# Four more head pairs of a sparse attention take their scores as side-by-side 64-row 32-bit matmuls, and the planner's constants are chosen anew

## The chip, the cores and the metric

The kernel runs on one core of one Trainium2 chip. The metric is device time in microseconds (us), as the median of several executions. The profile is of one execution on that core.

## What is computed

An attention with a threshold, followed by two feed-forward layers:

```python
scores = (q @ k.T) / sqrt(64)                      # 4 batches, 8 heads, 576 tokens, 64 wide
thresh = max(scores) - tau                         # per row
attn   = softmax(where(scores >= thresh, scores, -1e9))
x      = heads of (attn @ v) side by side          # 2304 tokens x 512
g      = relu(x @ w1_in) ** 2                      # 512 -> 2048
x      = g @ w1_out                                # 2048 -> 512
h      = x @ w2_in
out    = max(0.01 * h, h) @ w2_out
```

All arrays are 32-bit floats. With `tau` = 0.02 a score that lies just at the threshold decides whether an attention weight is kept, so the scores have to be nearly exact; that is why they are either taken as true 32-bit matmuls or from numbers split in a high and a low part.

## The kernel before, in words

The kernel writes all its work down as operations with the values they read and write (`op`, line 83), each with a due time `prio` and one or more engines that could do it, each at a cost in us. `order` (line 118) then simulates the engines once, ahead of the run, and so fixes the order of the instructions on every engine. Engine letters are T (TensorE), V (VectorE), A (ScalarE), G (GpSimd), S (the DMA queue on SyncE). Among the operations that could start, the one with the earliest due time is taken; an operation marked urgent keeps others from starting just before it; the weights `CFG["price"]` (line 190), one set for each stretch of the plan, say when an operation is left for another engine. On the chip each engine takes its instructions strictly in that order and waits by semaphores.

**Attention.** The 4 batches have 4 pairs of heads each, so there are 16 pairs (0 to 15), and every pair has 9 steps: four row tiles of 128 queries for each of the two heads, and one step for the last 64 queries of both heads. That makes 144 steps. `prep(n)` (line 465) loads pair n's queries, keys and values during pair n-1. `step(i)` (line 561) makes the 128 x 576 scores `s` in PSUM (two buffers for `s`; line 580 or 594), then, on the tile:

- line 602, VectorE: the row maximum, negated (`nb`); line 604, VectorE or GpSimd: the threshold `th`
- line 603, ScalarE: `e` = exp(s - max)
- line 609, VectorE: `e` = (s >= th) * e with the row sum; with it the PSUM buffer of `s` comes free
- lines 612 and 615: the reciprocal `r` of the sum

and `rest` (line 618) turns `e` into weights and transposes them. For pairs 0 to 3 (`nav`, not changed) this is a 32-bit transpose on TensorE (lines 634, 635). For pairs 4 to 15 the weights become two 16-bit tiles, a rounded high part and the remainder, in one of two ways: a scaling straight to the high part and line 656 on VectorE for the remainder; or, for the steps that `CFG["lb"]` lists by batch (step number modulo 8), a scaling in place, a rounding (line 652) and a subtraction (line 653), which VectorE or GpSimd may do. A DMA then transposes both (line 662). `values` (line 675) multiplies with V (line 690, or 695 for `nav`) and writes `xs` to `x1d` in DRAM: with line 710 on VectorE, or, for the pairs that `CFG["xsg"]` names, with a ScalarE copy (707) and a GpSimd addition (708).

**Two ways to the scores.** `CFG["nat"]` lists the pairs that take the first one:

```python
# a pair in nat (line 571 ff.): 32-bit, the 64-wide contraction in half the rows of the array
for g in range(2):
    rows = slice(g * D, (g + 1) * D)
    nc.tensor.matmul(ps.get()[r, g, 0:S2], lhsT=o.q2()[rows, a, q], rhs=o.k2()[rows, a], start=True, stop=True)
# every other pair (line 591 ff.): round 32-bit halves, high and low queries in the 128 rows
ops = [(r, q, kk[hh]) for hh, r, q in lhs for kk in (o.KH, o.KL)]
for k, (r, q, kk) in enumerate(ops):
    nc.tensor.matmul(ps.get()[r, g, 0:S2], lhsT=o.Q.get()[:, q], rhs=kk.get()[:, g_(g)], start=k == 0, stop=k == len(ops) - 1)
```

In the first way the queries lie twice, in rows 0 to 63 and 64 to 127; the upper rows hold the first 288 keys, the lower rows the other 288, and the two matmuls of a step (four in the ninth step) run side by side in the two halves of the array. The preparation is one scaling of 128 x 576 keys. In the second way a step is four matmuls of 128 rows by 288 columns (eight in the ninth step), and the preparation scales 128 x 1152 keys in a `wraw` buffer (lines 451 and neighbours), rounds the queries (two operations) and subtracts for their low part (two on 64 rows), rounds the keys (two) and subtracts (two): one operation against nine, beside a small memset (line 502). Queries and keys of such a pair pass through two of the three `wraw` buffers.

**Feed-forward.** `ffn` (line 717) does the first layer for the first 1792 tokens in blocks of 256, with 12, 12, 12 and 10 of 16 weight blocks (`nf`), alongside the attention: lines 743 (h) and 769 (y) fill TensorE between the scores. It starts once batch 0 is done, behind step 36. After the attention, lines 1173 and 1215 do the rest of the first layer, and lines 1062 and 1140 the second layer in a form with fewer products. `w_block` (line 351) and `single` (line 880) load and decode the weights.

Of the kernel before, what the change touches and what calls it, by code (L numbers as in the profile page):

```python
# [24 lines left out]

CFG = dict(
    price=[{'V': 4.26, 'A': 2.141, 'G': 1.969},
           {'V': 2.149, 'A': 0.525, 'G': 0.657},
           {'V': 1.817, 'A': 0.791, 'G': 0.994},
           {'V': 4.978, 'A': 0.359, 'G': 0.535},  # L30
           {'V': 1.875, 'A': 0.851, 'G': 2.206},
           {'V': 2.958, 'A': 1.093, 'G': 2.527},
           {'V': 3.025, 'A': 1.378, 'G': 3.11}],
    lead1=0.194, xsg0=[0, 1], lbm=8, lb=[[0, 1, 4, 6, 7], [1, 5], [4], [3, 7]], xsm=4, xsg=[1], dq=0.417, xu=True, pqk=-3.957, pd1=2.075,
    pex=0.67, pd2=1.854, ph=3.829, pl=-2.392, hu=False, bg=5.522, lead=4.309, w0=25.544, wstep=1.281, fend=1.014, tol=0.2, hor=-0.199,
    xlead=5.334, nb=3, eb=4, pb=3, ptb=3, kvb=3, nat=[0, 1, 2, 3, 4, 5], nav=4, two=False, vb=2, tmb=1, gb=2, xb=1, w2step=-2.074,
    nf=[12, 12, 12, 10], wo=2.034, wold=[0, 9, 10, 14, 16], yal=40.688, xl2=28.416, xp=5, sp=2.529, ws=-2.249, ww=28.906, zc=3.11, th=0.368,
    x2l=3.836, sg0=2.669, sgstep=1.117, zb=1.278, zin=0.923, zout=0.928, slack=0.02, slackd=1.05, wrb=3, r1b=1, xrb=1,
)


# [1317 lines left out]
```

## Time and profile before

| | |
|---|---|
| median of 3 runs | 1014.09 us (1008.28 to 1015.57) |
| the profiled execution, its own time | 1012.67 us |
| its span, first to last instruction | 1010.8 us (1.9 us lie around it) |
| mean granted TensorE clock | 0.988 of full speed |
| busy, share of the span | TensorE 95%, VectorE 83%, ScalarE 70%, GpSimd 37% |

Busy time of TensorE is the time covered by records of matmuls. A record lasts longer than the matmul keeps the next one from starting: rows of line 743 and 769 have records of 0.28 us that start 0.12 us apart. What a matmul costs is therefore read from start to start. The starts of line 602, one for each step, date the steps: step 36 (pair 4) is at 102 us, pair 5 at 131.3, pairs 6 to 9 lie from 162.4 to 276.8, and the last step starts at 451.7.

### The profile page before, as it was taken

To read this page: it belongs to the slowest core of one execution; us is meant where nothing else is said; L and a number is where in the kernel's file an instruction comes from. 1 tells how busy PE (TensorE), PEld (TensorE's weight loads), DVE (VectorE), ACT (ScalarE), POOL (GpSimd) and SP (SyncE) were. 2 spreads that over 40 slices of the span, in tenths; PEclk is the share of its full clock that TensorE was granted. 3 is DMA by queue.
4 is the path that set the end of the run, shared out by engine and by line. 5 is a ranking of instruction groups with operands and counts; after the bars stand their busy time and mean duration, and the time that the engine had idled before them with its cause. 6 is when DMAs were issued, how large, how long until landed. Compare 5 with 4: busy or idle time off the path is not lost.

```text
span 1010.8 us, 20761 instructions
## 1 busy us (share of the span) xinstructions
PE 963.6 (95%) x7436; PEld 831.2 (82%) x7436; DVE 834.7 (83%) x1948; ACT 704.1 (70%) x1361; POOL 377.4 (37%) x467
## 2 busy tenths in 40 slices
PE   7888799998999999999999999999999999999997
PEld 3444478898999988999978898778888888888897
DVE  6899898888999888874666999799979859858766
ACT  4877888878788689975566998767737536446343
POOL 4788888886877688951400000000100000000000
PEclk7999799999999999999999999999999999999999
DMA  7556799998989877766665563530020020010000
GB/s 175 162 167 174 192 189 188 184 179 177 181 168 182 166 155 148 152 122 192 194 197 165 177 195 119 168 103 20 1 85 2 1 85 2 2 64 1 22 23 22
DMA packets 199351, 123.79 MB, mean 122 GB/s; under 512 B 156880, under 2 KB 176976, under 8 KB 199248
## 3 DMA queue, kind: packets, MB, share of 16 engines
q1 hardware_dynamic: 198800, 122.10, 50.7%
q8 instruction: 59, 0.97, 0.4%
q10 hardware_dynamic: 448, 0.36, 0.2%
q14 instruction: 44, 0.36, 0.1%
HBM read 72.75 MB, written 17.83 MB: 90 GB/s over the span
## 4 chain that ended last, share of the span: by engine, by line
PE 61%; DVE 17%; ACT 9%; issue 5%; DMA 5%; POOL 2%; SPq 0%; DVEq 0%; ACTq 0%; POOLq 0%
PE y L1140 8%; PE y L1062 7%; PE h L1140 7%; PE h L1062 7%; PE h L743 6%; PE h L1173 6%; PE y L1215 6%; PE y L769 5%; DVE e L609 3%; DVE P L656 3%; DMA PT<-P 3%; DVE nb L602 3%; PE s L594 2%; PE o L690 2%; ACT e L603 2%
## 5 line engine op out<-in xcount | busy, mean ns | idle before, releaser
L609 DVE SCALAR_TENSOR_TENSOR e<-s,th,e 128x576 f32<-128x576 f32 x144 | 116.6, 811 | 22.0 <-ACT e L603 18.1
L603 ACT ACTIVATE e<-s,nb 128x576 f32<-128x576 f32 x144 | 106.0, 740 | 27.1 <-DVE nb L602 17.9
L602 DVE TENSOR_REDUCE nb<-s 128x1 f32<-128x576 f32 x144 | 106.7, 747 | 15.5 <-PE s L580 7.8
L656 DVE SCALAR_TENSOR_TENSOR P<-e,r,P 128x576 f16<-128x576 f32 x86 | 86.4, 1011 | 5.3 <-POOL P L622 2.8
L903 POOL MEMSET yo<- 128x128 f32 x5 | 1.0, 206 | 201.1 <-DVE b L1070 88.7
L690 PE MATMUL o<-PT,V 128*128 128x320 f16 (+1 forms) x432 | 61.5, 287 | 5.1 <-DVE vbound L535 3.1
L594 PE MATMUL s<-KH,Q 128*128 128x288 f32 x200 | 59.2, 314 | 6.2 <-DVE e L609 5.3
L1089 ACT ACTIVATE b<-b 128x1024 f32<-128x1024 f32 (+1 forms) x40 | 38.8, 971 | 33.1 <-DVE b L329 33.0
L1140 PEld LDWEIGHTS <-gh 128*128 128x128 f16 x560 | 54.5, 98 | 6.1
L329 DVE TENSOR_TENSOR b<-b 128x256 f32<-128x256 f32 (+1 forms) x120 | 45.4, 390 | 14.9 <-ACT b L1089 14.3
L318 ACT CAST gh<-b 128x384 f16<-128x384 f32 (+1 forms) x78 | 44.0, 564 | 19.1 <-DVE b L329 18.5
L594 PE MATMUL s<-KL,Q 128*128 128x288 f32 x200 | 55.9, 294 | 0.0
L580 PE MATMUL s<-KH,Q 64*128 64x288 f32 (+1 forms) x240 | 43.0, 483 | 12.3 <-DVE e L609 5.2
L690 PEld LDWEIGHTS <-V 128*128 128x128 f16 x432 | 39.0, 98 | 17.0 <-issue 6.1
L329 DVE TENSOR_TENSOR gl<-b,gh 128x384 f16<-128x384 f32 x80 | 48.9, 615 | 0.2 <-ACT gh L318 0.2
L318 ACT CAST xh<-xr 128x512 f16<-128x512 f32 (+3 forms) x65 | 36.9, 580 | 16.5 <-DVE xr L329 14.7
L331 POOL TENSOR_TENSOR gl<-r,gh 128x512 fp32r<-128x512 f32 x31 | 42.3, 1366 | 12.7 <-DMA x1d<-xs 6.0
L623 ACT ACTIVATE P<-e,r 128x576 f16<-128x576 f32 x53 | 40.5, 770 | 9.1 <-DMA PT<-P 4.5
L318 ACT CAST gh<-r 128x512 fp32r<-128x512 f32 (+1 forms) x72 | 43.4, 603 | 4.8 <-DVE r L1181 3.6
L594 PEld LDWEIGHTS s<-KH,Q 128*128 128x128 f32 x200 | 37.7, 189 | 10.8 <-DVE e L609 4.2
L329 DVE TENSOR_TENSOR gl<-r,gh 128x512 fp32r<-128x512 f32 (+1 forms) x44 | 31.4, 715 | 14.9 <-ACT gh L318 14.7
L604 POOL TENSOR_SCALAR th<-nb,ca 128x1 f32<-128x1 f32 x70 | 32.5, 466 | 24.4 <-DVE nb L602 16.6
(1130 smaller groups left out, 3523.5 us busy)
## 6 DMA issues: line engine op xcount, KB each, us to landing
wraw<-w SPq DMA_DIRECT2D x64, 512.0 KB, 4.3
wraw<-qT SPq DMA_DIRECT2D x20, 288.0 KB, 4.1
wraw<-kT SPq DMA_DIRECT2D x20, 288.0 KB, 4.1
out<-yo SPq DMA_DIRECT2D x18, 256.0 KB, 2.3
VA<-vv SPq DMA_DIRECT2D x32, 128.0 KB, 2.9
x2d<-yo SPq DMA_DIRECT2D x16, 256.0 KB, 3.2
xr<-x2d SPq DMA_DIRECT2D x4, 1024.0 KB, 6.0
y1d<-ys SPq DMA_DIRECT2D x14, 256.0 KB, 2.7
```

Of the source, the lines that this page charges most:

```text
L318: alts.append(("A", act(n, psum), lambda: nc.scalar.copy(o(), i()), kind))
L329: alts.append(("V", dve(n), lambda: nc.vector.tensor_tensor(out=o(), in0=a(), in1=b(), op=alu), kind + "*"))
L594: nc.tensor.matmul(ps.get()[r, g, 0:S2], lhsT=o.Q.get()[:, q], rhs=kk.get()[:, g_(g)], start=k == 0, stop=k == len(ops) - 1)
L602: op(("V", 0.75, lambda: nc.vector.tensor_reduce(out=nb.get(), in_=pv(), axis=AX.XY, op=ALU.max, negate=True)), [ps], [nb], i + CFG["pd1"] ...
L603: op(("A", 0.74, lambda: nc.scalar.activation(e.get(), pv(), AF.Exp, bias=nb.get(), scale=1.0)), [ps, nb], [e], i + CFG["pex"], True)
L609: op(("V", 0.82, lambda: nc.vector.scalar_tensor_tensor(out=e.get(), in0=pv(), scalar=th.get(), in1=e.get(), op0=ALU.is_ge, op1=ALU.mult, ...
L656: op(("V", 0.8, lambda: nc.vector.scalar_tensor_tensor(out=lo(), in0=ev(), scalar=r_.get()[:, k:k + 1], in1=hi(), op0=ALU.mult, op1=ALU.su ...
L690: nc.tensor.matmul(ps.get()[:, 0:w], lhsT=o.V16.get()[:, k if k < NH else k - NH, h].rearrange("p a d -> p (a d)"), rhs=parts16(pt)[:, k, ...
L743: nc.tensor.matmul(ps.get()[:, i], lhsT=a.get()[:, kc * P:(kc + 1) * P], rhs=x.get()[:, kc], start=(i == 0 and q == 0 and kc == 0), stop=( ...
L1062: nc.tensor.matmul(ps.get()[:, 0:w], lhsT=half(wt)[:, ct + kc * P:ct + (kc + 1) * P], rhs=xt(k)[:, kc], start=fresh and q == 0, stop=q == ...
L1140: nc.tensor.matmul(y.get()[:, c * h:(c + 1) * h], lhsT=l, rhs=r, start=first and c == 0 and q == 0, stop=last and c == len(ks) - 1 and q == 2)
L1173: nc.tensor.matmul(ps.get()[:, 0:n], lhsT=a.get()[:, kc * P:(kc + 1) * P], rhs=x.get()[:, kc, 0:n], start=(q == 0 and kc == 0), stop=(q == ...
```

## The change

Only constants change. `nat` gets pairs 6, 7, 8 and 9 beside 0 to 5. `lb` lists other and more steps: of the 36 steps of batch 1, 18 instead of 9 subtract for the remainder; of batch 2, 13 instead of 4; of batch 3, 18 instead of 9. `xsg` is emptied, so that pair 1 of each of the batches 1 to 3 (four `xs` tiles each) uses line 710 as well. `hu` and `xu` are marks of urgency: the scaling of `e` becomes urgent, and the making of `xs` no longer is. The rest are due times, prices and tolerances of the planner. `nf`, the numbers of buffers and `nav` stay.

```diff
     price=[{'V': 4.26, 'A': 2.141, 'G': 1.969},
-           {'V': 2.149, 'A': 0.525, 'G': 0.657},
-           {'V': 1.817, 'A': 0.791, 'G': 0.994},
-           {'V': 4.978, 'A': 0.359, 'G': 0.535},
-           {'V': 1.875, 'A': 0.851, 'G': 2.206},
-           {'V': 2.958, 'A': 1.093, 'G': 2.527},
-           {'V': 3.025, 'A': 1.378, 'G': 3.11}],
-    lead1=0.194, xsg0=[0, 1], lbm=8, lb=[[0, 1, 4, 6, 7], [1, 5], [4], [3, 7]], xsm=4, xsg=[1], dq=0.417, xu=True, pqk=-3.957, pd1=2.075,
-    pex=0.67, pd2=1.854, ph=3.829, pl=-2.392, hu=False, bg=5.522, lead=4.309, w0=25.544, wstep=1.281, fend=1.014, tol=0.2, hor=-0.199,
-    xlead=5.334, nb=3, eb=4, pb=3, ptb=3, kvb=3, nat=[0, 1, 2, 3, 4, 5], nav=4, two=False, vb=2, tmb=1, gb=2, xb=1, w2step=-2.074,
-    nf=[12, 12, 12, 10], wo=2.034, wold=[0, 9, 10, 14, 16], yal=40.688, xl2=28.416, xp=5, sp=2.529, ws=-2.249, ww=28.906, zc=3.11, th=0.368,
-    x2l=3.836, sg0=2.669, sgstep=1.117, zb=1.278, zin=0.923, zout=0.928, slack=0.02, slackd=1.05, wrb=3, r1b=1, xrb=1,
+           {'V': 1.56, 'A': 0.549, 'G': 0.69},
+           {'V': 1.817, 'A': 0.676, 'G': 0.904},
+           {'V': 4.978, 'A': 0.394, 'G': 0.428},
+           {'V': 2.445, 'A': 1.111, 'G': 4.308},
+           {'V': 2.617, 'A': 1.326, 'G': 3.065},
+           {'V': 3.041, 'A': 0.959, 'G': 2.966}],
+    lead1=-0.042, xsg0=[0, 1], lbm=8, lb=[[0, 1, 5], [1, 2, 4, 5], [3, 4, 5], [1, 3, 6, 7]], xsm=4, xsg=[], dq=0.417, xu=False, pqk=-4.584,
+    pd1=2.433, pex=0.235, pd2=1.954, ph=3.475, pl=-2.289, hu=True, bg=5.492, lead=4.309, w0=25.652, wstep=1.281, fend=1.015, tol=0.058,
+    hor=-0.251, xlead=5.334, nb=3, eb=4, pb=3, ptb=3, kvb=3, nat=[0, 1, 2, 3, 4, 5, 6, 7, 8, 9], nav=4, two=False, vb=2, tmb=1, gb=2, xb=1,
+    w2step=-4.165, nf=[12, 12, 12, 10], wo=2.483, wold=[0, 9, 10, 14, 16], yal=40.777, xl2=26.257, xp=5, sp=3.532, ws=0.975, ww=27.843,
+    zc=4.079, th=0.367, x2l=3.492, sg0=2.218, sgstep=1.072, zb=0.976, zin=0.743, zout=0.764, slack=0.02, slackd=1.05, wrb=3, r1b=1, xrb=1,
 )
```

## Rows read from the trace of the kernel before

**Rows 1.** Busy time by stretch: PE, PEld, DVE, ACT, POOL (x instructions), PEclk, DMA share, GB/s.

```profile
0.00:102.00 102.00, 83.32 (x483) 42.88 (x484) 86.55 (x208) 74.21 (x125) 74.71 (x109) 0.93 0.62 170
102.00:131.30 29.30, 23.27 (x134) 14.90 (x133) 26.39 (x67) 23.84 (x42) 23.60 (x29) 0.83 0.87 201
131.30:162.40 31.10, 29.51 (x224) 24.19 (x222) 28.58 (x70) 26.76 (x49) 26.78 (x26) 1.00 1.05 194
162.40:276.80 114.40, 107.38 (x847) 101.00 (x846) 100.44 (x234) 94.62 (x176) 91.94 (x104) 1.00 0.94 177
276.80:451.70 174.90, 171.29 (x1376) 162.52 (x1374) 150.45 (x336) 143.77 (x264) 134.89 (x170) 1.00 0.82 157
451.70:1010.80 559.10, 548.81 (x4385) 485.70 (x4383) 442.29 (x1042) 340.93 (x709) 25.50 (x32) 1.00 0.26 84
```

**Rows 2.** The same view for line 602 alone: DVE busy, PEclk, DMA share, GB/s.

```profile
162.40:276.80 114.40, 26.73 (x36) 1.00 0.94 177
```

**Rows 3.** Waits of PE from 131.3 to 451.7 us: total us, times, longest us.

```profile
PE s L594 <- DVE e L609: 5.3, 13, 0.8
PE o L690 <- DVE vbound L535: 3.1, 3, 1.9
```

**Rows 4.** Waits of PE from 102 to 131.3 us.

```profile
PE s L580 <- DVE th L604: 3.3, 1, 3.3
```

**Rows 5.** Timeline of PE, a 64-row score step between feed-forward matmuls: start, us, instruction.

```profile
152.95 0.28 PE L769 MATMUL y<-gh,w4ol 128*128 128x256 f32 x1
153.16 0.76 PE L580 MATMUL s<-KH,Q 64*128 64x288 f32 x4
153.85 0.39 PE L769 MATMUL y<-gh,w4oh 128*128 128x256 f32 x1
154.07 0.28 PE L769 MATMUL y<-gl,w4oh 128*128 128x256 f32 x1
```

**Rows 6.** Timeline of PE, a split score step between feed-forward matmuls.

```profile
161.28 0.30 PE L594 MATMUL s<-KH,Q 128*128 128x288 f32 x1
...
161.68 0.29 PE L594 MATMUL s<-KL,Q 128*128 128x288 f32 x1
161.82 0.64 PE L743 MATMUL h<-xh,w9il 128*128 128x256 f32 x4
```

**Rows 7.** Timeline of PE, the ninth step of a pair in the 64-row form.

```profile
148.13 0.71 PE L580 MATMUL s<-KH,Q 64*64 64x288 f32 x8
149.11 0.70 PE L690 MATMUL o<-PT,V 128*128 128x320 f16 x4 [0.27 <-DMA PT<-P]
```

**Rows 8.** Groups by line and shape, preparation of split pairs: busy us, mean ns, idle before.

```profile
L451 ACT ACTIVATE wraw<-wraw,qsc 128x1152 f32<-128x1152 f32 x9 | 11.3, 1254 | 3.3 <-DMA wraw<-kT 3.3
L318 ACT CAST Q<-wraw 128x576 fp32r<-128x576 f32 x10 | 6.7, 669 | 0.1
L322 POOL TENSOR_SCALAR Q<-wraw 128x576 fp32r<-128x576 f32 x10 | 8.0, 805 | 0.2
L318 ACT CAST KH<-wraw 128x576 fp32r<-128x576 f32 x20 | 13.2, 665 | 0.0
L331 POOL TENSOR_TENSOR Q<-wraw,Q 64x576 fp32r<-64x576 f32 x17 | 25.0, 1474 | 1.3
L331 POOL TENSOR_TENSOR KL<-wraw,KH 128x576 fp32r<-128x576 f32 x17 | 26.5, 1556 | 1.9 <-ACT KH L318 1.3
```

**Rows 9.** The same view: remainder of the weights (656, 331) and `xs` (708, 710).

```profile
L656 DVE SCALAR_TENSOR_TENSOR P<-e,r,P 128x576 f16<-128x576 f32 x86 | 86.4, 1011 | 5.3 <-POOL P L622 2.8 <-ACT P L623 2.4
...
L331 POOL TENSOR_TENSOR P<-e,P 128x576 f16<-128x576 f32 x19 | 26.0, 1368 | 4.5 <-ACT P L318 4.0
...
L710 DVE SCALAR_TENSOR_TENSOR xs<-o,vback,tmp 64x320 f32<-64x320 f32 x18 | 9.7, 538 | 6.5 <-ACT tmp L705 6.5
L708 POOL TENSOR_TENSOR xs<-xs,tmp 64x320 f32<-64x320 f32 x10 | 9.7, 968 | 0.5 <-ACT xs L707 0.5
```

**Rows 10.** DMA issues: count, KB each, us to landing.

```profile
wraw<-kT SPq DMA_DIRECT2D x20, 288.0 KB, 4.1
```

## The prediction

> **What bounds the kernel now.** I read the busy time by stretch first [rows 1]. Behind 102 us TensorE is the fullest engine everywhere: from 131.3 to 162.4 us it lacks 31.1 - 29.5 = 1.6 us, over pairs 6 to 9 it lacks 114.4 - 107.4 = 7.0 us, from there to the last step 3.6 us, and in the 559 us behind the attention 10.3 us, under 2%. The reader is to see that the time behind 131 us is TensorE's own work plus some 22 us of gaps, so every microsecond of work added to TensorE is paid in full, and only a closed gap pays it back. Ahead of 102 us it is otherwise: TensorE lacks 18.7 us and VectorE is busy 86.6 of 102; there is no feed-forward to fill with yet. Pair 4 (102 to 131.3 us) stands between: 6.0 us without a matmul and a granted clock of 0.83.
>
> The waits say whose the gaps are. From 131.3 us on, the largest is the split scores waiting for line 609, which frees their PSUM buffer: 13 times, 5.3 us; next the V products waiting for the bound on V, 3.1 us [rows 3]. In pair 4 it is one wait of 3.3 us for line 604 [rows 4]. All are VectorE being late, at 88% busy in pairs 6 to 9 (100.4 of 114.4 us). These 36 steps are 36 calls of line 602 [rows 2].
>
> **TensorE's part, step by step.** A split step costs what lies between its first matmul and the next other one: 161.82 - 161.28 = 0.54 us, or 0.133 us for each of its four [rows 6]. For a 64-row step the neighbours have to be counted too. The last feed-forward matmul ahead starts at 152.95 and would let the next start at 153.07; the scores start at 153.16, 0.09 late. They hold the array until 153.85, 0.69 us. The next feed-forward matmul needs 0.22 us to the start of its successor instead of 0.12, so 0.10 more [rows 5]. Together 0.88 us against 0.54: plus 0.34 us a step. The ninth step takes 149.11 - 148.13 = 0.98 us, of which 0.27 us is marked as a wait for a DMA [rows 7], plus 0.09 ahead; in the split form it is eight matmuls of 0.133 us, 1.06 us. I take no difference there, with a bound of 0.3 us less each. So TensorE gets 32 x 0.34 = 11.0 us more work in pairs 6 to 9, where it is the bound. The low end is 8 us (below), and 1 us less for the ninth steps.
>
> The 0.19 us at the two edges of a 64-row step stand in the rows without a cause. The Trainium skill, TensorEngine Tiling (Array Packing), section Key Properties, says that changing the tiling mode, and not merely the tile, drains TensorE. The edges agree with that in place and sign. By this rule the price hangs on the order: two 64-row steps run back to back pay the edges once.
>
> If the new due times (`pqk` moves the scores 0.63 steps earlier) set all 32 steps in such pairs, 16 x 0.19 = 3.0 us of the 11.0 go. I keep 11.0, because the step in the rows stands alone [rows 5], and 8.0 as the low end.
>
> **The other engines' part.** Each split pair's preparation is, from its rows [rows 8]: ScalarE 1.25 for the keys' scaling, 0.67 for a query tile, 2 x 0.67 for the keys, together 3.3 us; GpSimd 0.81 for the other query tile, 17/10 x 1.47 and 17/10 x 1.56 for the subtractions, together 6.0 us (VectorE has the other three of each 20). The one scaling that stays is half as wide as the 1.25 us one, so about 0.7 us. Four pairs thus free 4 x 8.6 = 34 us: some 24 on GpSimd, 10 on ScalarE, almost none on VectorE.
>
> The new `lb` spends that. 27 more steps subtract instead of using line 656: VectorE loses 27 x 1.01 = 27 us, GpSimd gains up to 27 x 1.37 = 37 us, and 27 roundings at about 0.67 us (the row of a cast of that size [rows 8]) fall to ScalarE, 18 us [rows 9]. The empty `xsg` gives VectorE 12 x 0.54 = 6 us back and takes 12 x 0.97 = 12 us from GpSimd, and 6 us of copies, taken as long as line 710's, from ScalarE. The balance: VectorE about -21 us, GpSimd +1, ScalarE +2. VectorE carried 279 us from 131.3 to 451.7 us, so it falls from 87% to 81%. This is the part that can pay: the waits were on VectorE.
>
> What is moved on the queues is small. Keys of four pairs come as 2 x 144 instead of 2 x 288 KB [rows 10], 1.2 MB less, 6 us at 177 GB/s in a stretch whose DMA share is 0.94; no large wait of TensorE there is for a load. The scores are an added weight at the head of TensorE's queue: a step that waits for its `s` buffer holds up all the feed-forward matmuls behind it, and they in turn line 750 and what follows. A longer score step itself lies inside a step period of 114.4 / 36 = 3.2 us, with two buffers, and is covered.
>
> **Gaps closed.** Pairs 5 to 9 have 8.6 us of them; I take two thirds, 5.7 us (bounds 0 and 8.6), since both the preparation and part of line 656 go there. From 276.8 to 451.7 us 3.6 us; half, 1.8 us (bounds 3.6 closed, 2 more). In pair 4 6.0 us, half, 3.0 us (6 closed, 3 more): nothing of its own work goes except half of `lb`, but one wait of 3.3 us for an ill-placed instruction is what a new order can remove or make. Ahead of 102 us the work is the same and only due times and urgency differ; VectorE leaves 15.5 us, and I take 2 us gained (6 gained, 4 lost). Behind 451.7 us, with new due times for weights and for the second layer, I take nothing (5 either way, half of the 10.3 us there).
>
> **Sum.** +11.0 - 5.7 - 1.8 - 3.0 - 2.0 = -1.5 us on the profiled execution's 1012.67 us, so 1011.2. That execution lies 1.4 us under the median of the runs, 1014.09; on the median's scale 1012.6. I give 1012. About 1% (10 us) is what a measurement of this kernel can tell from no change, so this is none.
>
> **Rivals.**
> - *The dearer scores are paid and nothing comes back.* VectorE is relieved, yet the score steps still find their PSUM buffer taken, because line 609 waits for ScalarE's exponential as before, or GpSimd's 37 us of subtractions come late to the DMA transposes. For: GpSimd was busy 92 of 114 us and gets no lighter in sum. Against: the largest wait is of VectorE. Then 1014.1 + 11.0 = 1025, up to 1028 with the new gaps of 2 or 3 us bounded above. It decides over 1% once less than 1 us is won in all stretches together.
> - *The relief reaches everything.* Gaps of pairs 5 to 9 fall by 7.5 us, of pairs 10 to 15 by 2.9, pair 4's by 4.8 and the start gains 6: 11.0 - 21.2 = -10.2, so 1004; with scores in couples, 8.0 instead of 11.0, and the second half 3 us better, 998. For: all waits named above are VectorE's, which loses 21 us. Against: it needs nearly every gap closed, and the start is not touched by `nat`.
> - *Score steps run in couples.* The edges are paid once for two steps: 8.0 instead of 11.0, about 1009.6. For: `pqk` is earlier, and there are two `s` buffers. Against: line 609 frees them one at a time, about a step apart. This is what the drain of the Trainium skill's Key Properties would come to.
> - *The second half decides.* `w2step`, `ws`, `zc` and `zin` move the decoding of weights behind 451.7 us; up to 5 us of the 10.3 us there either way, 1007 to 1018. For: VectorE is busy 442 of 559 us. Against: TensorE is full there with two layers' matmuls, and these stay the same.
>
> **How the numbers follow.** The forecast has 0.44, dearer scores unpaid 0.18, relief everywhere 0.26, couples 0.05, the second half 0.07. The first, fourth and fifth lie within 1%: 0.56; faster by over 1%: 0.26; slower by over 1%: 0.18. The forecast's own range is 1005 to 1020; to hold 8 in 10 it is taken to 998 and 1027, into both outer cases.
>
> **What would show it.** In the changed profile, line 580 has 400 instead of 240 records and line 594 120 instead of 200 for each of KH and KL; a 64-row step between feed-forward matmuls shows 0.69 us and the two late starts; line 656 has 59 calls; VectorE is at or under 81% between steps 45 and 143. Pairs 6 to 9 should take 114.4 us plus 11 less what their gaps lose, if the same feed-forward work lies in them. I am wrong if the time moves by over 10 us; in a faster run the start or pair 4 should be shorter, in a slower one the waits of line 580 on line 609 should be as long as those of line 594 were.

## The result, and the profile after

The changed kernel takes 1017.6 us (median of 11 runs), the kernel before 1008.3 (11 runs): ratio 1.0087, 95% interval 1.0064 to 1.0110, so slower by some 8.8 us (the two medians differ by 9.3). The forecast was no change, with 1012, 1.5 us faster than the time it started from; the step lies within the 1% that was named, but it is clear of the noise and in the other direction.

The profiled execution of after has 1017.5 us and a span of 1015.7, 4.9 more than before's profiled one. The view is the busy time by stretch of after, with the same columns and the same steps as in [rows 1] (steps 0 to 35, pair 4, pair 5, pairs 6 to 9, pairs 10 to 15, the rest).

```profile
0.00:99.70 99.70, 80.05 (x483) 41.52 (x484) 86.07 (x207) 74.29 (x125) 74.93 (x110) 0.97 0.64 173
99.70:130.20 30.50, 22.18 (x137) 14.12 (x138) 27.67 (x65) 24.38 (x46) 23.64 (x29) 0.89 0.81 193
130.20:160.60 30.40, 29.50 (x222) 23.67 (x220) 26.63 (x64) 24.45 (x46) 25.70 (x25) 1.00 0.92 186
160.60:275.90 115.30, 112.04 (x838) 89.77 (x837) 91.65 (x220) 91.14 (x166) 84.29 (x108) 1.00 0.91 174
275.90:453.30 177.40, 169.52 (x1344) 160.49 (x1343) 141.70 (x335) 146.47 (x267) 140.63 (x168) 0.99 0.79 148
453.30:1015.70 562.40, 553.25 (x4422) 489.66 (x4420) 438.04 (x1034) 346.06 (x723) 26.05 (x34) 1.00 0.27 84
```

Beside [rows 1], pairs 6 to 9, where the change sits, take 115.3 instead of 114.4 us, with 9 matmul records fewer (838 against 847, about 1.1 us): the dearer scores cost some 2 us there, and TensorE's time without a record falls from 7.0 to 3.3 us. Most of the loss is elsewhere. Pairs 10 to 15, whose scores are taken as before, need 177.4 instead of 174.9 us, with 7.9 us of gaps against 3.6 and 32 matmuls fewer (1344 against 1376); what they leave undone stands in the last stretch, 562.4 instead of 559.1 us, with 37 matmuls more. VectorE is lighter, as forecast, 91.7 instead of 100.4 us in pairs 6 to 9 and 141.7 instead of 150.5 behind; that did not help.

The step itself reads as forecast. The timeline of TensorE in after, a 64-row step of pair 7 and a ninth step of pair 9:

```profile
222.15 0.64 PE L743 MATMUL h<-xh,w9il 128*128 128x256 f32 x4
222.72 0.76 PE L580 MATMUL s<-KH,Q 64*128 64x288 f32 x4
223.41 0.39 PE L769 MATMUL y<-gh,w6oh 128*128 128x256 f32 x1
223.63 0.28 PE L769 MATMUL y<-gl,w6oh 128*128 128x256 f32 x1
...
263.31 0.71 PE L580 MATMUL s<-KH,Q 64*64 64x288 f32 x8
263.96 0.39 PE L769 MATMUL y<-gh,w2oh 128*128 128x256 f32 x1
264.18 0.28 PE L769 MATMUL y<-gl,w2oh 128*128 128x256 f32 x1
```

The fourth matmul of line 743 starts at 222.15 + 3 x 0.12 = 222.51 and would let the next go at 222.63; the scores start 0.09 later, hold the array 0.69 us, and the matmul behind them needs 0.10 more: 0.88 us again. A ninth step holds it 0.65 us; the rows show its edge behind, 0.10 us again, and with 0.09 taken for the one ahead it comes to 0.84, under the 1.06 of the split form. The added work is 32 x 0.34 - 4 x 0.22 = 10.0 us.

Who is waited for in pairs 10 to 15 is in the waits of TensorE, first after, then before in its stretch from 276.8 to 451.7 us:

```profile
PE s L594 <- DVE e L609: 5.8, 7, 1.7
PE o L690 <- DVE vbound L535: 1.1, 2, 0.8
```

```profile
PE s L594 <- DVE e L609: 1.9, 5, 0.7
PE o L690 <- DVE vbound L535: 1.2, 2, 0.8
```

It is the same wait for line 609, seven times instead of five and longer on average. The longest can be followed in the timeline of after (start, us, engine, instruction, idle before and its releaser):

```profile
355.69 0.67 POOL L322 TENSOR_SCALAR P<-e 128x576 f16<-128x576 f32 x1 [0.38 <-ACT e L623]
...
356.34 0.87 POOL L604 TENSOR_SCALAR th<-nb,ca 128x1 f32<-128x1 f32 x1
356.40 0.76 DVE L329 TENSOR_TENSOR P<-e,P 128x576 f16<-128x576 f32 x1 [1.74 <-POOL P L322]
...
357.24 0.82 DVE L609 SCALAR_TENSOR_TENSOR e<-s,th,e 128x576 f32<-128x576 f32 x1
...
358.22 0.37 PE L594 MATMUL s<-KH,Q 128*128 128x288 f32 x1 [1.73 <-DVE e L609]
```

GpSimd has the rounding of one tile (line 322) ahead of the threshold of another (604); VectorE has that tile's subtraction (329) ahead of line 609. So VectorE idles 1.74 us for a rounding, line 609 starts behind the subtraction and behind the threshold, and TensorE stands 1.73 us with all its feed-forward work behind the score. VectorE and TensorE both stand idle for a while in the same few microseconds: the order in the queues does it.

Such a wait can cost more than its length. The busy time of after ahead of this wait, around it, behind it and further on (columns as above):

```profile
349.60:356.20 6.60, 6.26 (x50) 5.94 (x49) 4.58 (x10) 6.05 (x10) 3.93 (x7) 1.00 1.06 214
356.20:359.60 3.40, 1.68 (x14) 1.50 (x13) 2.69 (x8) 2.19 (x7) 3.17 (x7) 1.00 0.40 124
359.60:363.00 3.40, 3.40 (x16) 2.62 (x15) 2.05 (x5) 2.79 (x6) 3.37 (x4) 0.50 0.03 5
363.00:369.80 6.80, 6.80 (x57) 6.25 (x55) 5.62 (x15) 6.02 (x12) 5.46 (x6) 1.00 1.00 179
```

For 3.4 us behind it the granted clock is 0.50, the lower of TensorE's two levels (1.2 and 2.4 GHz); at half speed that is about 1.7 us of work, an estimate, and the records hide it, since TensorE counts as busy throughout. Before has 1.00 in every stretch behind 131.3 us [rows 1]. Not every wait is followed by such a fall: behind one of 1.66 us at 271.7 us in after the clock stays at 1.00. For pairs 10 to 15 the count comes out with it: 32 matmuls fewer at 0.12 us and 2.5 us more time are 6.3 us, against 4.3 us of new gaps and 1.7 us of clock.

### The profile page after: what moved, and what is told of

It reads as the page before. It is cut to its first block, busy times and chain, and to the rows that moved or that the text cites. A ratio compares the mean times of both kernels' runs of the same rounds, so it can differ in the third digit from the quotient of the medians.

```text
span 1015.7 us, 20710 instructions
## 1 busy us (share of the span) xinstructions
PE 966.5 (95%) x7436; PEld 819.2 (81%) x7436; DVE 811.8 (80%) x1916; ACT 706.8 (70%) x1368; POOL 375.3 (37%) x471
## 4 chain that ended last, share of the span: by engine, by line
PE 46%; DVE 7%; ACT 3%; issue 2%; POOL 1%; DMA 1%; DVEq 0%; ACTq 0%; POOLq 0%
PE y L1140 8%; PE y L1062 7%; PE h L1140 7%; PE h L1062 7%; PE y L1215 5%; PE h L1173 5%; PE y L769 3%; PE h L743 2%; DMA y1d<-ys 1%; PE o L690 1%; DVE gl L329 1%; DVE yo L1225 1%; DVE xl L329 0%; DVE yo L1149 0%; DVE r L1181 0%
## 5 line engine op out<-in xcount | busy, mean ns | idle before, releaser
L580 PE MATMUL s<-KH,Q 64*128 64x288 f32 (+1 forms) x400 | 68.8, 462 | 16.2 <-DVE e L609 12.1
L331 POOL TENSOR_TENSOR gl<-r,gh 128x512 fp32r<-128x512 f32 (+1 forms) x34 | 44.1, 1298 | 58.5 <-ACT gh L318 56.6
L656 DVE SCALAR_TENSOR_TENSOR P<-e,r,P 128x576 f16<-128x576 f32 x59 | 56.6, 963 | 7.5 <-ACT P L623 4.4
L331 POOL TENSOR_TENSOR P<-e,P 128x576 f16<-128x576 f32 x45 | 58.2, 1297 | 11.4 <-ACT P L318 10.6
L318 ACT CAST gh<-b 128x384 f16<-128x384 f32 x80 | 45.2, 565 | 20.9 <-DVE b L329 20.5
L580 PEld LDWEIGHTS s<-KH,Q 64*128 64x128 f32 (+1 forms) x400 | 28.5, 180 | 35.1 <-issue 16.7
L318 ACT CAST xh<-xr 128x512 f16<-128x512 f32 (+3 forms) x62 | 35.2, 581 | 13.6 <-DVE xr L329 12.2
L623 ACT ACTIVATE e<-e,r 128x576 f32<-128x576 f32 x49 | 37.4, 772 | 8.4 <-DVE r L615 8.3
L1070 DVE TENSOR_TENSOR b<-h,b 128x256 f32<-128x256 f32 (+1 forms) x96 | 35.4, 374 | 7.9 <-PE h L1062 5.8
L594 PE MATMUL s<-KH,Q 128*128 128x288 f32 x120 | 35.7, 315 | 6.0 <-DVE e L609 5.8
L329 DVE TENSOR_TENSOR gl<-r,gh 128x512 fp32r<-128x512 f32 (+1 forms) x41 | 29.0, 710 | 14.5 <-ACT gh L318 14.4
```

The source lines that it names most:

```text
L318: alts.append(("A", act(n, psum), lambda: nc.scalar.copy(o(), i()), kind))
L329: alts.append(("V", dve(n), lambda: nc.vector.tensor_tensor(out=o(), in0=a(), in1=b(), op=alu), kind + "*"))
L331: alts.append(("G", pool2(n), lambda: nc.gpsimd.tensor_tensor(out=o(), in0=a(), in1=b(), op=alu), kind))
L656: op(("V", 0.8, lambda: nc.vector.scalar_tensor_tensor(out=lo(), in0=ev(), scalar=r_.get()[:, k:k + 1], in1=hi(), op0=ALU.mult, op1=ALU.su ...
```

## The experiments

Time of TensorE without a record, by stretch (length less PE busy, as in the view above; each stretch is bounded by the same steps), and the ratio to before with its interval. "64-row pairs" counts the pairs in that form.

| run | 64-row pairs | pair 4 | pair 5 | 6 to 9 | 10 to 15 | rest | ratio |
|---|---|---|---|---|---|---|---|
| before | 6 | 6.0 | 1.6 | 7.0 | 3.6 | 10.3 | 1 |
| the change | 10 | 8.3 | 0.9 | 3.3 | 7.9 | 9.2 | 1.0087 (1.0064 to 1.0110) |
| e1 | 10 | 6.3 | 1.1 | 5.8 | 8.8 | 10.4 | 1.0118 (1.0087 to 1.0150) |
| e2 | 6 | 4.8 | 0.6 | 7.8 | 9.4 | 14.2 | 1.0183 (1.0148 to 1.0218) |
| e3 | 10 | 6.6 | 0.1 | 3.4 | 6.9 | 10.5 | 1.0140 (1.0110 to 1.0170) |
| e4, order of before | 6 | 6.3 | 1.8 | 1.9 | 4.6 | 10.0 | 1.0038 (1.0015 to 1.0061) |
| e5, order of before | 6 | 5.8 | 1.7 | 6.5 | 3.6 | 9.0 | 0.9992 (0.9963 to 1.0022) |
| e6, order of before | 10 | 6.0 | 1.1 | 3.5 | 3.6 | 9.5 | 1.0014 (0.9990 to 1.0038) |
| e7 | 6 | 7.2 | 1.7 | 8.5 | 7.8 | 9.1 | 1.0090 (1.0058 to 1.0123) |
| e8 | 10 | 7.5 | 3.2 | 7.3 | 9.3 | 9.2 | 1.0214 (1.0179 to 1.0248) |
| e9 | 6 | 6.0 | 1.3 | 8.5 | 11.2 | 9.0 | 1.0122 (1.0085 to 1.0159) |
| e10 | 6 | 6.0 | 1.4 | 6.4 | 13.0 | 9.4 | 1.0098 (1.0060 to 1.0136) |
| e11 | 6 | 6.7 | 2.6 | 7.3 | 8.2 | 12.7 | 1.0126 (1.0090 to 1.0161) |
| e12 | 10 | 6.1 | 0.7 | 8.0 | 10.9 | 9.5 | 1.0164 (1.0126 to 1.0201) |

**The two halves of the change, and one list.** Edit of e1, from before:

```diff
-nat=[0, 1, 2, 3, 4, 5]
+nat=[0, 1, 2, 3, 4, 5, 6, 7, 8, 9]
```

> The constants of before, and only pairs 6 to 9 in the 64-row form. Theory A (TensorE pays 3.3 us of matmuls and 6.3 us at the edges, and the lighter preparation closes about 8 us of gaps in these pairs, as counted from start to start in the two traces): ratio to before 1.0016, between 0.998 and 1.005, gaps of pairs 6 to 9 down from 13.6 to about 6 us, pairs 10 to 15 unchanged at 11 us. Theory B (the 64-row form is what costs, the constants are harmless): ratio 1.007 to 1.010.

Edit of e2, from after:

```diff
-nat=[0, 1, 2, 3, 4, 5, 6, 7, 8, 9]
+nat=[0, 1, 2, 3, 4, 5]
```

> All new constants, but pairs 6 to 9 stay in the split form. Theory A (the loss is from the constants, which open about 6 us of gaps behind pair 9): ratio to before about 1.007, between 1.004 and 1.011, gaps of pairs 10 to 15 at 16 us or more against 11. Theory B (constants harmless): 0.997 to 1.002.

Edit of e3, from after:

```diff
-lb=[[0, 1, 5], [1, 2, 4, 5], [3, 4, 5], [1, 3, 6, 7]]
+lb=[[0, 1, 4, 6, 7], [1, 5], [4], [3, 7]]
```

> The changed kernel with the old list of steps that subtract for the remainder, so 86 calls of line 656 instead of 59. Theory A in its narrow form (the 27 moved steps make the new gaps of pairs 10 to 15): ratio to before about 1.003, gaps of pairs 10 to 15 back at 11 to 12 us. If due times and urgency make them: 1.008 to 1.010, gaps as in the changed kernel (17 us). If taking work from VectorE did help: above 1.011.

(The gaps in these three expectations, 13.6 or 11 us, were counted from start to start of matmuls; the table counts time without a record, so only their differences compare.) Neither half alone is faster than both together: the constants alone, 1.0183, are slower than the change's 1.0087, and the 64-row form alone, 1.0118, is no better, though the two intervals overlap. Together the halves would make 1.030: the two parts do not add. Theory B of e1 has its 1.007 to 1.010 inside e1's interval, but the constants are not harmless (e2); theory A of e2 has its new gaps about right, 9.4 against 3.6 us, and not its time. In e1 the gaps of pairs 10 to 15 grow as in the change (the row below against 3.6 us in [rows 1]), although no constant is new; in e3 the time with the old list is 1.0140, where only work taken from VectorE to some use was expected above 1.011. But e3 too has another order than the change, and its trace doesn't put the loss where most of the moved steps lie: pair 5 starts 6.4 us later than in after (136.6 against 130.2 us), and the whole span is 6.1 us longer (1021.8 us). So e3 doesn't show what the list is worth. What all three share with the change is that the planner makes a new order for every engine.

```profile
276.70:457.60 180.90, 172.12 (x1374) 162.78 (x1373) 150.74 (x330) 142.22 (x261) 138.85 (x178) 1.00 0.79 149
```

**The price alone, in the old order.** Edit of e4, from before (the planner's cost stays, so no instruction changes its place):

```diff
+                if 6 <= n <= 9:
+                    r, q, kk = ops[0]
+                    nc.tensor.matmul(ps.get()[r, g, 0:S2], lhsT=o.Q.get()[:, q], rhs=kk.get()[:, g_(g)], start=True, stop=True)
                 for k, (r, q, kk) in enumerate(ops):
```

> Before, with one more matmul of 128 rows by 288 columns ahead of each half of a score tile in pairs 6 to 9, overwritten at once: 72 matmuls of 0.133 us, 9.6 us of TensorE work, as much as the 64-row form adds, with the preparation and the planned order unchanged. If TensorE is the bound there: plus 9.6 us, ratio 1.009 to 1.010. If its gaps take the work in: below 1.004.

Just inside the lower expectation, with an interval that reaches beyond it: 9.6 us of work cost 0.38%, 3.8 us (interval 1.5 to 6.2). The stretch of pairs 6 to 9 has 72 matmuls more, 116.60 us, and 1.9 us of gaps instead of 7.0:

```profile
157.50:274.10 116.60, 114.66 (x919) 109.59 (x919) 99.08 (x237) 94.11 (x176) 90.39 (x104) 1.00 0.91 174
```

The added work went into gaps in which TensorE had waited for VectorE: from 130 to 455 us the split scores wait 1.5 us for the instruction of line 609 (line 612 in e4) instead of 5.3.

**The relief alone, and the whole step, in the old order.** Edit of e5 and e6, from before, shortened (`quiet` keeps an operation in the plan and issues nothing):

```diff
+    def quiet(alts):
+        return [(g, c, lambda: None, *k) for g, c, _, *k in alts]
-                op(sub(lambda h=h: qs(h)[D:P], ...), [qr, Q], [Q], at(3 + h))
+                low = sub(lambda h=h: qs(h)[D:P], ...)
+                op(quiet(low) if 6 <= n <= 9 else low, [qr, Q], [Q], at(3 + h))
...
+# e5: the high part of the keys once more in place of the low one
+ops = [(r, q, kk[hh]) for hh, r, q in lhs for kk in (o.KH, o.KH if 6 <= n <= 9 else o.KL)]
+# e6: 32-bit copies instead of the roundings, and for each half g of the keys
+nc.tensor.matmul(ps.get()[r, g, 0:S2], lhsT=o.Q.get()[rows, q:q + r.stop - r.start], rhs=f32(o.KH[hh].get())[rows, g_(g)], start=True, stop=True)
```

> Before in its own order, without the subtractions for the low parts of queries and keys in pairs 6 to 9 (the high parts of the keys stand in for the low ones, so the low part of these scores is left out): 13 or 14 fewer instructions of about 1.5 us on GpSimd and 2 or 3 on VectorE, TensorE's work as before. If the preparation's load held TensorE up: 2 to 5 us faster, ratio 0.995 to 0.998. If it lay beside other work: 0.999 to 1.001.

> Before, with the planner run as before, so that every instruction keeps its place; in pairs 6 to 9 the two roundings become plain 32-bit copies, the two subtractions of queries and of keys are not issued, and each score tile is taken by two 64-row 32-bit matmuls from these copies. It has the TensorE price of the change (about 9.6 us), part of its relief, and no new order. If the loss comes from the new order of all engines: close to the run with 72 more matmuls, ratio 1.000 to 1.004, and far under the 1.0118 of the 64-row form in a new order. If the 64-row form itself costs it (by its edges, which also hold up what is behind): 1.009 or more.

Without the subtractions GpSimd is busy 76.0 instead of 91.9 us in pairs 6 to 9, and nothing comes of it: ratio 0.9992 with 1 in its interval, gaps of 6.5 against 7.0 us. With the 64-row scores besides, in the old order, the ratio is 1.0014, with 1 in its interval. The busy time of e5 in pairs 6 to 9, and of e6 in pairs 6 to 9 and 10 to 15:

```profile
165.00:278.40 113.40, 106.90 (x845) 100.61 (x845) 96.94 (x233) 94.60 (x176) 75.96 (x95) 1.00 0.95 180
```

```profile
161.50:278.80 117.30, 113.76 (x848) 91.12 (x848) 97.18 (x232) 94.40 (x176) 74.74 (x95) 1.00 0.91 174
278.80:453.50 174.70, 171.13 (x1375) 162.50 (x1374) 149.52 (x336) 143.40 (x264) 134.68 (x170) 1.00 0.80 157
```

In e6 pairs 6 to 9 take 2.9 us more than before, with half the gaps; pairs 10 to 15 are before's to 0.2 us. This is the 64-row form of the change without its order, and it costs nothing that can be measured. e1 differs from it in its order, and in a preparation that is lighter still (one scaling, no copies); the lighter preparation can hardly cost, so the new order is what is left for the difference between 1.0014 and 1.0118. The change's new `lb` and empty `xsg` were not tried in the old order.

**Another order alone.** Edits of e7, e9 and e10, each from before; all three keep the operations and let the planner choose order and, where there is a choice, engine anew:

```diff
-            op(("T", 0.69, tiles), [o.Q, o.KH[0]], [ps], i + CFG["pqk"], True)
+            op(("T", 0.88, tiles), [o.Q, o.KH[0]], [ps], i + CFG["pqk"], True)
...
-pqk=-3.957
+pqk=-3.9
...
-lead=4.309
+lead=4.2
```

> Before, with nothing changed but the planner's cost of a 64-row score step, 0.88 instead of 0.69 us: the same instructions in another order on every engine. If before's constants fit its own plan so closely that another order costs by itself: ratio 1.005 to 1.015, with gaps of TensorE spread over many pairs. If the order hardly matters: 0.998 to 1.003.

> Before with one due time moved: the scores 0.06 steps later (pqk -3.9 instead of -3.957). The same instructions, another order. If before sits at an order that its constants were fitted to, a step off it costs: ratio 1.002 to 1.008. If orders differ by chance around it, either sign: 0.996 to 1.004.

> Before with another due time moved: the V products 0.11 steps earlier (lead 4.2 instead of 4.309). As for the due time of the scores: fitted order, 1.001 to 1.007; chance, 0.996 to 1.004.

All three are about 1% slower, 9 to 12 us, with the same work; e9 and e10 lie beyond even what a fitted order was expected to lose (e10's interval reaches back into it). A due time moved by six hundredths of a step costs about as much as the whole change did. The gaps open in the same place, and in good part by the same wait: in pairs 10 to 15 line 609 holds the split scores up for 4.8, 6.1 and 6.0 us in e7, e9 and e10, against 1.9 in before. Pairs 10 to 15 of e7, e9 and e10, and the first wait of TensorE in e9 from 100 to 460 us (before has 5.3 us of it [rows 3]):

```profile
280.10:459.70 179.60, 171.80 (x1368) 162.02 (x1367) 151.31 (x334) 141.59 (x265) 138.17 (x170) 1.00 0.79 153
```

```profile
277.40:461.10 183.70, 172.53 (x1365) 161.90 (x1363) 157.37 (x332) 140.18 (x259) 139.65 (x179) 1.00 0.77 149
```

```profile
275.20:462.80 187.60, 174.63 (x1371) 164.92 (x1370) 155.99 (x324) 140.14 (x259) 141.51 (x185) 0.98 0.77 146
```

```profile
PE s L594 <- DVE e L609: 9.4, 16, 1.7
```

In e9 and e10 VectorE is busy 157.4 and 156.0 us here, with 332 and 324 instructions; before it was 150.5 us with 336 [rows 1]. Part of that is line 656, 46 calls in each; its row for pairs 10 to 15 in before, e9 and e10 (count, busy us, mean ns), and what lies ahead of e10's longest wait:

```profile
L656 DVE SCALAR_TENSOR_TENSOR P<-e,r,P 128x576 f16<-128x576 f32 x46 | 44.6, 976 | 3.3 <-POOL P L622 1.7 <-ACT P L623 1.6
L656 DVE SCALAR_TENSOR_TENSOR P<-e,r,P 128x576 f16<-128x576 f32 x46 | 50.3, 1101 | 3.5 <-ACT P L623 2.1 <-POOL P L622 1.3
L656 DVE SCALAR_TENSOR_TENSOR P<-e,r,P 128x576 f16<-128x576 f32 x46 | 51.0, 1114 | 2.7 <-ACT P L623 2.4 <-POOL P L622 0.3
```

```profile
420.37 0.87 POOL L708 TENSOR_TENSOR xs<-xs,tmp 64x320 f32<-64x320 f32 x1 [0.16 <-ACT xs L707]
420.57 3.87 DVE L656 SCALAR_TENSOR_TENSOR P<-e,r,P 128x576 f16<-128x576 f32 x1
421.20 1.41 POOL L331 TENSOR_TENSOR V<-VA,V 128x640 f16<-128x640 f32 x1
422.57 1.26 POOL L331 TENSOR_TENSOR xl<-xr,xh 128x512 fp32r<-128x512 f32 x1
425.36 0.40 PE L594 MATMUL s<-KH,Q 128*128 128x288 f32 x1 [1.94 <-DVE e L609]
```

The call has a record of 3.87 us, against a median of 0.82 in e10, while GpSimd runs three two-operand instructions back to back; line 609 stands behind it. So a new order changes not only what stands ahead of what, but also what runs beside what, and with it how long the same call takes. That GpSimd's neighbours are what lengthens it was not tested by itself; the planner reckons with something of the kind (`locks`, line 158). In the change itself this adds little: there the mean of line 656 in pairs 10 to 15 is 989 ns against 976.

**A true cost for the planner.** Could the loss come from planning with 0.69 us for a step that takes 0.88? Edit of e8, from after, is the line of e7; e11 (six pairs, from before) and e12 (ten pairs, from after) have it too, with all due times, prices and lists chosen again for the smallest end on the planner's own clock.

> The changed kernel with the planner's cost of a 64-row score step at the measured 0.88 us instead of 0.69, so the plan of pairs 0 to 9 no longer runs ahead of the chip. If the mispriced step is what spoils the new order: ratio to before 0.998 to 1.004. If any order for which the constants were not chosen is worse: 1.010 to 1.020, above the 1.0087 of the change.

> Six pairs in the 64-row form as before, the planner's cost of such a step at the measured 0.88 us, and its constants chosen anew for the planner's own clock (995.7 us against 997.7 for before, which counts the step at 0.69). If the loss of the change comes from an order planned with a step that is too cheap, an order planned with its true price is as good as before or better: ratio 0.992 to 1.000. If the planner's clock says little of the chip: 1.003 to 1.015, as for any other order.

> Ten pairs in the 64-row form, as the change has them, the planner's cost at 0.88 us, and its constants chosen anew (its clock: 1004.5 us, against 1011.8 for the changed constants at that cost). If the order is what costs and the true price mends it: between 1.001 and 1.006, under the 1.0087 of the change, and above the run with six pairs by some of the 9.6 us of TensorE work. If the planner's clock says little: 1.008 to 1.020.

The price is not it: 1.0214, 1.0126 and 1.0164, none at or under the change's 1.0087 (e11's interval overlaps with it). The planner's clock puts e11 2 us ahead of before; the chip puts it 13 us behind. It does not see differences of this size. No run was measurably faster than before.

## Why the prediction was wrong

The step that failed is the one from VectorE's load to TensorE's gaps behind pair 5: work taken from VectorE, 21 us in the balance, was to close half the gaps of pairs 10 to 15, and the sum had no term for what a new order costs by itself.

- *TensorE's 11.0 us more work.* Right: 0.88 us a step was found again (32 x 0.34 is 10.9), and the ninth step is 0.22 us cheaper where no difference was taken; 10.0 us. The edges of 0.09 and 0.10 us come back in after. The Trainium skill, TensorEngine Tiling (Array Packing), Key Properties, says that a change of tiling mode drains TensorE, and the edges agree with that in place and sign.
- *The bound.* Here the reasoning failed first, though to the other side: "every microsecond of work added to TensorE is paid in full". In the order of before, 9.6 us cost 3.8 (e4), and the whole step with its relief 1.4 us (e6, interval -1.0 to 3.8). Work added to TensorE fell into gaps in which it had waited for VectorE (the waits for line 609 shrink, above). And the sum mixed two measures, the price of a step from start to start and the gaps as time without a record: in e4 pairs 6 to 9 grow by 2.2 us for 9.6 us of work, so 7.4 us were taken in, while the time without a record falls by 5.1.
- *Gaps of pairs 5 to 9, 5.7 us closed.* The size was nearly right, 8.6 to 4.2 us, and that is luck, for the reason was wrong: the relief alone closes next to nothing (e5: 8.6 to 8.2), the added work alone closes 4.9 us (e4: 8.6 to 3.7).
- *Gaps of pairs 10 to 15, 1.8 us closed; pair 4, 3.0 us closed.* These are the terms that turned the sign: 4.3 us opened and 2.3 us opened. In pairs 10 to 15 some 1.7 us of the lower clock behind a wait come on top. I had VectorE's load fall from 87% to 81% and read the gaps as its load. VectorE did get lighter, 150.5 to 141.7 us in pairs 10 to 15. The one wait that was followed is a matter of which instruction stands ahead of line 609, at 356 us above, and that is redrawn by any change of the plan; the others were not followed one by one.
- *The start, 2.0 us gained.* The profile shows 102.0 to 99.7 us, but e4, e5 and e6, whose order is before's, have 99.3, 102.0 and 103.6: executions of one order differ by more there, so nothing of it can be put down to the change. The same holds for the length of pair 4, 30.5 us in after and 27.2 to 31.6 in these four. Behind it one can compare: from pair 5 to the end after takes 885.5 us, 6.0 more than before's 879.5. Before's profiled execution was also above the median of its runs (1012.7 against 1008.3), so the rest of the 8.8 us can't be placed. The forecast's 1012 started from the median of three runs, 1014.1, which 11 runs put at 1008.3; that 1017.6 lies inside its 1005 to 1020 is luck as well.
- *The second half, nothing.* It took 3.3 us more, 4.4 us more of TensorE's busy time less 1.1 us of gaps: the feed-forward work that pairs 10 to 15 had left over (37 matmuls at 0.12 us).
- *The rivals.* "The dearer scores are paid and nothing comes back" came nearest in time and is not the mechanism: much came back where the scores are, and about as much was lost where the form of the scores had not changed. Couples of score steps hardly occur: one is seen in pairs 6 to 9 of after, at 234.0 us. That a new order costs by itself was among no rivals; it stood only in bounds of 2 to 5 us on single stretches.

Shown: the 64-row form is neutral in the old order (e6), and three other orders of the old work cost about 1% each (e7, e9, e10). That the change's 0.87% is the cost of its order is argued from these by subtraction, not shown. Open are the moved steps of `lb` and the emptied `xsg`, which bring GpSimd and ScalarE other work and were only run in new orders; the 64-row form in after's own order; and which of the due times set the bad places, since none can be moved without a new order. That before's constants were fitted on the chip is not known here either; that three small moves away from them (e7, e9, e10) all lost is what speaks for it.

## What to carry to other kernels

When a static plan has been fitted on the chip, price an edit in two parts: the work, and the loss of the fit; the second can be measured beforehand by moving one due time a little and timing the kernel, and here it was 1%, more than the work. To judge the work itself, keep the old order: leave operations in the plan that issue nothing, or add instructions that the plan doesn't see. And a gap is not the load of the engine that ends it; read which instruction stood in front of the releasing one, and what ran beside it.

## What was not expected of the hardware

In a stretch where TensorE had records 94% of the time [rows 1], 9.6 us more of its work cost 3.8 us. After one wait of 1.73 us TensorE ran at half its full clock for 3.4 us. The same 46 calls of one VectorE instruction took 44.6 us in one order and 51.0 in another. And runs of one kernel with one order spread from 1005.0 to 1015.6 us, as much as the effect that was sought; with 11 runs each it was told apart. The profiled executions suggest where they spread: in before's order the first 36 steps and pair 4 took 131.3, 126.5, 133.6 and 130.9 us (before, e4, e5, e6), with a granted clock of 0.83, 0.94, 0.75 and 0.91 in pair 4. The edits of e4 to e6 act only behind that.
